# Twelve strided units normalised on GpSimd, and turn and values one unit step later

## The chip, the cores and the metric

One Trainium2 chip, one NeuronCore of it. The metric is the device time in microseconds (us) of one execution, as the median of several runs. Engines are named as the profile names them: PE (TensorE matmuls), PEld (its weight loads), DVE (VectorE), ACT (ScalarE), POOL (GpSimd), and the DMA queues that an engine issues to (SPq, ACTq, POOLq).

## The reference

Attention over 8 batches, 8 heads, 576 positions and 64 dimensions, then a mixture of 8 experts with one expert per token. All data is float32.

```
scores = (q @ k.T) / sqrt(64)
heads 0-3: key j is seen by query i if 0 <= i - j < 32             (local)
heads 4-7: key j is seen if j <= i and j % 32 == i % 32            (strided)
attn = exp(scores - max) / (sum + 1e-9);  x = attn @ v             (4608 tokens x 512)
logits = x @ w_gate + modality_bias[modality_id]
expert = argmax(logits);  gate = softmax(logits)[expert]
out = gate * (relu(x @ w1[expert]) @ w2[expert])                   (512 -> 1024 -> 512)
```

## The kernel before

The kernel has two stages on one core. The attention stage writes the 4608 rows of x to DRAM and works out where each token belongs; the expert stage gathers tokens in slots of 256 and runs the two expert layers on each slot.

**Units.** Attention is cut into 32 units that alternate: even units are local (one head of two batches), odd units are strided (two heads of one batch). Strided units count their own index from 0 to 15, so `self.n` of a strided unit is k for the unit 2k+1 of the loop. A unit goes through five parts:

- `load` and `load_values` (SP's queue, issued in program order, each made to follow a PE instruction named in `at`): q and k, then v.
- `prep` (local only): q is copied into a padded tile `qd`, one half by DVE, one half by ACT (L326).
- `masks` and `scores`: PE writes the mask and adds the score products in PSUM. DVE takes the maximum and subtracts it (L353 and L354 for local, L454 and L455 for strided), ACT takes the exponential (L355 and L356; L456). For a strided unit DVE then sums (`sms`, L458), adds 1e-9 (L459), takes the reciprocal (L460) and multiplies the exponentials by it into `en` (L462). Local units are divided after the value product instead.
- `turn`: PE transposes the exponentials (`ex` of a local unit, `en` of a strided one) and ACT copies them to SBUF (`et`, L368 and L371; `eb`, L471).
- `values`: PE multiplies by v. For a local unit DVE adds 1e-9, takes the reciprocal and scales into `xt` (L392 to L398); for a strided one ACT copies into `xc` (L491).

**The unit loop.** PE's instructions are kept in the order in which they are written (`manual_schedule`). Step n of the loop writes: masks and scores of unit n, turn of unit n-2, values of unit n-3, the loads of later units in between, `prep` of unit n+2, one store of finished rows (`store_rows`, a POOL DMA of L498 that is kept in order with the other POOL DMAs), and five pieces of the `extra` work (`pop(POPS)`): transposes of a finished pair of batches, its routing, and the slot tables. The other engines' orders are set by a planner that lists instructions by program order and by when it reckons them ready. An engine executes its list in order.

**Buffers.** PSUM is a ring of eight banks (`pa`). `ex`, `exs`, `sms`, the loaded tiles and `eb` have two buffers each, `et` one, and the `en` tiles two, kept by hand in `ens` because their padding is zeroed once by POOL.

After the loop the local pool is released and the expert stage's tiles are laid over it. Its slots are gathered by POOL's indirect DMAs and its weights are converted by ACT and DVE beside the matmuls of L940 and L954.

Of the kernel before, what the change touches and what calls it, by code (L numbers as in the profile page):

```python
# [11 lines left out]
F32 = mybir.dt.float32  # L12
# [5 lines left out]
ALU = mybir.AluOpType  # L18
AX = mybir.AxisListType

P = 128
# [51 lines left out]
def _place(g, jj):  # L73

    return 16 + jj if g == 8 else 4 * (g // 2) + g % 2 + 2 * jj
# [7 lines left out]
def _residues(half, a, j):  # L83

    return (16 * half + 6 * a + 3 * j, 3) if a < 2 else (16 * half + 12 + 2 * j, 2)
# [106 lines left out]
def attention_moe(ctx: ExitStack, tc: tile.TileContext, a, out):  # L192
    nc = tc.nc
# [15 lines left out]
    def keep_busy(n, name):  # L209
        t = pa(name)  # L210
        for _ in range(n):
            nc.tensor.matmul(t, idle[:, 0:P], idle[:], start=True, stop=True)  # L212
# [11 lines left out]
    at = {"scores": None, "turn": None, "values": None}  # L224
# [63 lines left out]
    lp = lp_cm.__enter__()  # L288


    def zeros(n, shape, name):
        return [lp.tile(shape, F32, bufs=1, name=f"{name}{i}") for i in range(n)]

    qds = zeros(2, [P, 18, 2, 32], "qd")
    ets = zeros(1, [P, 18, 2, 32], "et")
    ens = zeros(2, [P, 12, 64], "en")
    for t in qds + ets:
        nc.vector.memset(t[:], 0.0)
    for t in ens:
# [3 lines left out]
    class Local:  # L303
# [34 lines left out]
        def scores(self):  # L338
            n, qk, qd = self.n, self.qk, self.qd
            mx = lp.tile([P, 9], F32, tag="mx", name=f"mx{n}")  # L340
            self.ex = ex = lp.tile([P, 11, 64], F32, tag="ex", name=f"ex{n}")
            for g0, gn, s in self.ss:
                for g in range(gn):
                    for jj in range(2):
                        i = _place(g0 + g, jj)
                        at["scores"] = nc.tensor.matmul(  # L346
                            s[64 * jj:64 * jj + 64, g, :],
                            qd[:, i, :, :].rearrange("p b q -> p (b q)"),
                            qk[:, 18 + i:20 + i, :].rearrange("p b q -> p (b q)"),
                            start=False, stop=True, skip_group_check=True,  # L350
                        )
                m = mx[:, g0:g0 + gn]
                nc.vector.tensor_reduce(m, s, AX.X, ALU.max)  # L353
                nc.vector.tensor_tensor(ex[:, g0:g0 + gn, :], s, m.unsqueeze(2).to_broadcast([P, gn, 64]), ALU.subtract)  # L354
                nc.scalar.activation(ex[:, g0:g0 + 4, :], ex[:, g0:g0 + 4, :], AF.Exp, scale=0.125)  # L355
            nc.scalar.activation(ex[:, 9:11, :], ex[:, 8:9, :].to_broadcast([P, 2, 64]), AF.Exp, scale=0.125)  # L356
# [46 lines left out]
    class Strided:  # L403
# [30 lines left out]
        def scores(self):  # L434
            n, qk = self.n, self.qk
            for sl in range(6):
                for j in range(2):
                    r0, nr = _residues(sl % 2, sl // 2, j)
                    w, c = 18 * nr, slice(18 * r0, 18 * r0 + 18 * nr)
                    for h in range(2):  # L440
                        r = slice(64 * h, 64 * h + 64)
                        at["scores"] = nc.tensor.matmul(
                            self.s[h][64 * j:64 * j + w, 54 * sl:54 * sl + w], qk[r, 0, c], qk[r, 1, c],
                            start=False, stop=True, skip_group_check=True,
                        )
            mx = lp.tile([P, 12], F32, tag="mxs", name=f"mxs{n}")
            ex = lp.tile([P, 12, 54], F32, tag="exs", name=f"exs{n}")

            def bc(t, k):
                return t.unsqueeze(2).to_broadcast([P, k, 54])  # L450

            for h in range(2):
                s3, g = self.s[h].rearrange("p (i k) -> p i k", i=6), slice(6 * h, 6 * h + 6)
                nc.vector.tensor_reduce(mx[:, g], s3, AX.X, ALU.max)  # L454
                nc.vector.tensor_tensor(ex[:, g, :], s3, bc(mx[:, g], 6), ALU.subtract)  # L455
            nc.scalar.activation(ex[:], ex[:], AF.Exp, scale=0.125)  # L456
            sm = lp.tile([P, 12], F32, tag="sms", name=f"sms{n}")
            nc.vector.tensor_reduce(sm[:], ex[:], AX.X, ALU.add)  # L458
            nc.vector.tensor_scalar(sm[:], sm[:], 1e-9, None, ALU.add)  # L459
            nc.vector.reciprocal(sm[:], sm[:])  # L460
            self.en = ens[n % 2]
            nc.vector.tensor_tensor(self.en[:, :, 0:54], ex[:], bc(sm, 12), ALU.mult)  # L462

        def turn(self):
            n = self.n
# [29 lines left out]
    def store_rows():  # L495
        if rows:
            dst, src = rows.pop(0)
            pin(nc.gpsimd.dma_start(dst, src))  # L498

    def finish_pair(bp, xt, xcs):  # L500

        def rows_of(c, k0):
            kn = min(4, 9 - k0)
            t = pa(f"xs{bp}{c}{k0}").rearrange("p (g q) -> p g q", g=4)
            for k in range(kn):
                turned_to(t[:, k, :], xcs[2 + c][:, P * (k0 + k):P * (k0 + k + 1)])
            nc.scalar.copy(xt[:, k0:k0 + kn, 256 + P * c:256 + P * c + P], t[:, :kn, :])  # L507

        def columns_of(c, k0):
            kn = min(4, 9 - k0)  # L510
            t = pa(f"xl{bp}{c}{k0}").rearrange("p (g q) -> p g q", g=4)
            for k in range(kn):
                turned_to(t[:, k, :], xt[:, k0 + k, P * c:P * c + P])
            nc.scalar.copy(xcs[c][:, P * k0:P * (k0 + kn)], t[:, :kn, :].rearrange("p g q -> p (g q)"))

        def store(k, kn):
            r0 = T2 * bp + P * k
            rows.append((xd[r0:r0 + P * kn, :].rearrange("(k p) c -> p k c", p=P), xt[:, k:k + kn, :]))

        for c in range(2):  # L520
            for k0 in (0, 4, 8):
                yield
                columns_of(c, k0)
        routing = route(bp, xt, xcs)
        next(routing)
        next(routing)
        for k0 in (0, 4, 8):
            for c in range(2):
                next(routing, None)
                yield  # L530
                rows_of(c, k0)
                if k0 and c == 0:
                    store(k0 - 2, 2)
            store(k0, min(2, 9 - k0))
        yield from routing
# [448 lines left out]
    units, ends = [], {}  # L984
# [10 lines left out]
    def after(bp, xt, xcs):  # L995
        yield from finish_pair(bp, xt, xcs)
        yield
        for ph, (last_bp, _) in enumerate(PHASES):
            if bp == last_bp:
                yield from slots(ph)  # L1000

    extra = []

    def pop(k):
        for _ in range(k):
            while extra and next(extra[0], extra) is extra:
                extra.pop(0)
# [15 lines left out]
    def look_up(k):  # L1023
        if k == len(plan):
            found[k] = half_entries()
        if k < len(plan) and plan[k][1] in tables:
            n, t, s, xrows = plan[k]
            found[k] = entries(n, tables[t][0], s, xrows)
# [13 lines left out]
    nu = len(units)  # L1042
# [4 lines left out]
            units[i].prep()  # L1047
    man = tc.manual_schedule(engines={mybir.EngineType.PE})
    man.__enter__()
    for n in range(nu + 3):  # L1050
        paced = n >= PACED

        if not paced:
            for part in range(2):
                if n + 3 < nu:
                    units[n + 3].load(part, None)
            for part in range(2):
                if 1 <= n <= nu:
                    units[n - 1].load_values(part, None)
        if n in FILL:  # L1060
            keep_busy(FILL[n], f"warm{n}")
        if paced and n + 3 < nu:
            units[n + 3].load(0, at["values"])
        if n < nu:
            units[n].masks()
            units[n].scores()
        if paced and n + 3 < nu:
            units[n + 3].load(1, at["scores"])
        if 2 <= n <= nu + 1:
            units[n - 2].turn()  # L1070
        if paced and n <= nu:
            units[n - 1].load_values(0, at["turn"])
        if n >= 3:
            units[n - 3].values()
            if n - 3 in ends:
                extra.append(after(*ends[n - 3]))
        if paced and n <= nu:
            units[n - 1].load_values(1, at["values"])
        if n == SETUP:
            routing_setup()  # L1080
        if n + 2 < nu:
            units[n + 2].prep()
        store_rows()
        pop(POPS)
        for i in range(2):
            if n == nu - 4:
                look_up(i)
            if n == nu - 3:
                gather(i)
            if n == nu - 2:  # L1090
                load(0, i)
        if n == nu + 1:
            turn(0)
    man.__exit__(None, None, None)
    lp_cm.__exit__(None, None, None)
# [68 lines left out]
```

## Time and profile before

| what | value |
| --- | --- |
| median of 3 runs | 603.1 us (601.81 to 607.35) |
| the profiled execution, and its span | 602.83 us, 601.0 us |
| granted clock, mean | 0.993 |
| busy share of the span | PE 94%, PEld 83%, DVE 74%, ACT 65%, POOL 42% |
| moved by DMA | 102.46 MB, mean 170 GB/s |

A busy share is a mean over both stages. A row of the stretches view gives, for a stretch of the span, the busy time of each engine; a row of the timeline gives start, duration, engine, line, tiles and, in brackets, how long the engine sat idle before it and what ended that. In the timeline rows that are merged, xN counts the instructions.

### The profile page before, as it was taken

What the parts mean: (1) busy time and instruction counts of PE and PEld (TensorE: products, weight loads), DVE (VectorE), ACT (ScalarE), POOL (GpSimd) and SP (SyncE); (2) the same over time, 40 slices, a digit from 0 to 9 for tenths busy, and PEclk for the clock granted to TensorE, in tenths of its full rate; (3) what the DMA queues carried; (4) which work ended last, traced back from release to release, by engine and by line L of the source; (5) the groups of instructions that cost most, each with busy time, mean ns of one, the idle gap of its engine ahead of it and who ended that gap; (6) DMA issues with size and microseconds to landing.
All of it is one profiled execution on the core that took longest, in us unless ns stands there. A gap on an engine that the chain in (4) does not pass through costs nothing.

```text
span 601.0 us, 15492 instructions
## 1 busy us (share of the span) xinstructions
PE 565.7 (94%) x6107; PEld 498.5 (83%) x6109; DVE 446.8 (74%) x1076; ACT 388.6 (65%) x798; POOL 250.4 (42%) x226
## 2 busy tenths in 40 slices
PE   8777899797899999999999999999999999999995
PEld 4666787676669999999999999999999999999994
DVE  7867886985968799666787787787787787787542
ACT  4767877765796666776665575575665665665652
POOL 0011011117237537555645645645645646532310
PEclk9999899999999999999999999999999999999998
DMA  8984997998844944744754743313214239413621
GB/s 311 299 259 152 335 316 257 322 306 273 267 115 164 219 168 105 217 170 106 177 210 106 219 167 93 71 36 105 72 37 106 70 116 277 111 40 72 228 103 41
DMA packets 73572, 102.46 MB, mean 170 GB/s; under 512 B 48531, under 2 KB 48787, under 8 KB 69908
## 3 DMA queue, kind: packets, MB, share of 16 engines
q0 software_dynamic: 20672, 58.01, 28.6%
q1 hardware_dynamic: 52340, 42.87, 26.8%
q8 instruction: 50, 0.82, 0.6%
q10 hardware_dynamic: 480, 0.51, 0.3%
q14 instruction: 30, 0.25, 0.1%
HBM read 123.85 MB, written 19.18 MB: 238 GB/s over the span
## 4 chain that ended last, share of the span: by engine, by line
PE 82%; ACT 7%; DVE 6%; issue 3%; POOL 0%; another core or an unknown queue 0%; POOLq 0%; ACTq 0%
PE h L940 34%; PE o L954 33%; PE o L382 2%; PE s L346 2%; PE ot L483 1%; ACT xc L491 1%; PE lg L543 1%; PE xs L227 1%; PE ts L227 1%; DVE ex L354 1%; DVE mx L353 1%; DVE sms L458 1%; PE t L227 1%; PE warm L212 1%; ACT et L368 1%
## 5 line engine op out<-in xcount | busy, mean ns | idle before, releaser
L976 DVE TENSOR_TENSOR wl<-raw,wh 128x512 fp32r<-128x512 f32 x288 | 187.7, 691 | 64.2 <-ACT wh L975 55.2
L975 ACT CAST wh<-raw 128x512 fp32r<-128x512 f32 x288 | 163.9, 619 | 66.6 <-PE o L954 43.1
L940 PE MATMUL h<-xh,wl 128*128 128x256 f32 x576 | 162.7, 283 | 0.0
L940 PE MATMUL h<-xl,wh 128*128 128x256 f32 x576 | 162.6, 283 | 0.0
L940 PE MATMUL h<-xh,wh 128*128 128x256 f32 x576 | 162.4, 282 | 0.1
L822 POOL DMA_INDIRECT raw<-in_w,wi x72 | 95.9, 1332 | 156.3 <-DVE wl L976 117.6
L940 PEld LDWEIGHTS h<-xh,wh 128*128 128x128 f32 x576 | 109.5, 190 | 7.5 <-issue 0.6
L940 PEld LDWEIGHTS h<-xl,wh 128*128 128x128 f32 x576 | 109.6, 190 | 5.5
L954 PE MATMUL o<-wh,hh 128*128 128x512 f32 x288 | 114.2, 396 | 0.0
L954 PE MATMUL o<-wl,hh 128*128 128x512 f32 x288 | 113.8, 395 | 0.0
L940 PEld LDWEIGHTS h<-xh,wl 128*128 128x128 f32 x576 | 109.7, 190 | 1.4 <-DVE wl L976 0.4
L954 PE MATMUL o<-wh,hl 128*128 128x512 f32 x288 | 110.5, 391 | 0.0
L943 ACT ACTIVATE hh<-h 128x256 fp32r<-128x256 f32 x144 | 55.4, 385 | 71.1 <-PE h L940 46.7
L945 DVE SCALAR_TENSOR_TENSOR hl<-h,hh 128x256 fp32r<-128x256 f32 x144 | 60.7, 421 | 33.3 <-ACT hh L943 21.6
L954 PEld LDWEIGHTS o<-wh,hl 128*128 128x128 f32 x288 | 53.5, 188 | 11.0
L954 PEld LDWEIGHTS o<-wh,hh 128*128 128x128 f32 x288 | 54.6, 189 | 7.6
L954 PEld LDWEIGHTS o<-wl,hh 128*128 128x128 f32 x288 | 54.6, 190 | 5.6
L962 POOL DMA_INDIRECT out<-y,le x36 | 44.7, 1242 | 20.6 <-ACT y L961 11.0
L806 POOL DMA_INDIRECT fx<-xd,le x36 | 40.1, 1113 | 11.9 <-issue 10.7
L813 POOL DMA_INDIRECT le<-ld,li x36 | 39.4, 1095 | 12.9 <-issue 10.1
L498 POOL DMA_DIRECT2D xd<-xt x20 | 14.5, 727 | 62.3 <-ACT xt L507 62.3
L382 PE MATMUL o<-vv,et 128*64 128x65 f32 x512 | 22.7, 231 | 5.5 <-issue 3.3
(189 smaller groups left out, 749.1 us busy)
## 6 DMA issues: line engine op xcount, KB each, us to landing
vv<-in_vl SPq DMA_DIRECT2D x32, 292.5 KB
qks<-in_qks SPq DMA_DIRECT2D x32, 288.0 KB
xd<-xt POOLq DMA_DIRECT2D x16, 512.0 KB
qk<-in_qkl SPq DMA_DIRECT2D x16, 304.0 KB
qk<-in_qkl SPq DMA_DIRECT2D x16, 288.0 KB
vs<-in_vs SPq DMA_DIRECT2D x32, 144.0 KB
raw<-in_w,wi POOLq DMA_INDIRECT x72
xd<-xt POOLq DMA_DIRECT2D x4, 256.0 KB
```

The costliest lines, as they stand in the source:

```text
L227: at["turn"] = nc.tensor.transpose(dst, src, ident)
L382: at["values"] = nc.tensor.matmul(o[64 * jj:64 * jj + 64, k, :], et[:, u, :, :].rearrange("p g q -> p (g q)"), vv[:, u, :], start=True, st ...
L806: pin(nc.gpsimd.indirect_dma_start(xt[:, h, :], None, xd[0:xrows, :], IOA(ap=le[:, h, 0:1], axis=0)))
L813: pin(nc.gpsimd.indirect_dma_start(le[:, h, :], None, ld[0:xrows, :], IOA(ap=li[:, s, h:h + 1], axis=0)))
L822: pin(nc.gpsimd.indirect_dma_start(raws[j].rearrange("p f c -> p (f c)"), None, a["w"], IOA(ap=wi[:, s, j:j + 1], axis=0), bounds_check=E ...
L940: nc.tensor.matmul(hp, w[:, a1], x[:, c, :], start=(k == 0), stop=(k == 11))
L943: nc.scalar.activation(hh[:], hp, AF.Relu)
L945: nc.vector.scalar_tensor_tensor(hl[:], hp, 0.0, hh.bitcast(F32), ALU.max, ALU.subtract)
L954: nc.tensor.matmul(os[h], hx[:, m], w[:, 512:1024], start=(f == 0 and i == 0), stop=(f == 7 and i == 2))
L962: outs.add(pin(nc.gpsimd.indirect_dma_start(out, IOA(ap=le[:, h, 0:1], axis=0), y[:], None, bounds_check=NT - 1, oob_is_err=False)))
L975: nc.scalar.copy(wh[:, c], raw[:, c])
L976: nc.vector.tensor_tensor(wl[:, c], raw[:, c], wh[:, c].bitcast(F32), ALU.subtract)
```

## The change

Four things are edited. The multiplication into `en` (L462) goes to GpSimd for the strided units whose index is under 12 (loop units 1 to 23) and stays on VectorE for the last four. In step n the loop turns unit n-3 instead of n-2, multiplies by the values of unit n-4 instead of n-3, and loads the values of unit n-2 instead of n-1. The loop has one more step (36 instead of 35), and the turn of the first expert slot moves with it. `en` and the local `ex` have three buffers instead of two.

```
-    ens = zeros(2, [P, 12, 64], "en")
+    ens = zeros(3, [P, 12, 64], "en")
...
-            self.ex = ex = lp.tile([P, 11, 64], F32, tag="ex", name=f"ex{n}")
+            self.ex = ex = lp.tile([P, 11, 64], F32, tag="ex", bufs=3, name=f"ex{n}")
...
-            self.en = ens[n % 2]
-            nc.vector.tensor_tensor(self.en[:, :, 0:54], ex[:], bc(sm, 12), ALU.mult)
+            self.en = ens[n % 3]
+            (nc.gpsimd if n < 12 else nc.vector).tensor_tensor(
+                self.en[:, :, 0:54], ex[:], bc(sm, 12), ALU.mult)
...
-    for n in range(nu + 3):
+    for n in range(nu + 4):
...
-                if 1 <= n <= nu:
-                    units[n - 1].load_values(part, None)
+                if 2 <= n <= nu + 1:
+                    units[n - 2].load_values(part, None)
...
-        if 2 <= n <= nu + 1:
-            units[n - 2].turn()
-        if paced and n <= nu:
-            units[n - 1].load_values(0, at["turn"])
-        if n >= 3:
-            units[n - 3].values()
-            if n - 3 in ends:
-                extra.append(after(*ends[n - 3]))
-        if paced and n <= nu:
-            units[n - 1].load_values(1, at["values"])
+        if 3 <= n <= nu + 2:
+            units[n - 3].turn()
+        if paced and n <= nu + 1:
+            units[n - 2].load_values(0, at["turn"])
+        if n >= 4:
+            units[n - 4].values()
+            if n - 4 in ends:
+                extra.append(after(*ends[n - 4]))
+        if paced and n <= nu + 1:
+            units[n - 2].load_values(1, at["values"])
...
-        if n == nu + 1:
+        if n == nu + 2:
             turn(0)
```

## Rows read from the trace of the kernel before

**Rows 1.** Stretches: busy PE, PEld, DVE, ACT, POOL; clock, DMA share, GB/s.
```profile
8.00:34.00 26.00, 20.87 (x603) 17.41 (x604) 22.10 (x58) 19.18 (x42) 1.13 (x4) 1.00 0.91 294
...
34.00:58.00 24.00, 18.29 (x431) 14.46 (x429) 16.72 (x45) 15.81 (x36) 1.52 (x3) 1.00 0.71 226
58.00:127.00 69.00, 60.02 (x1584) 51.81 (x1580) 58.09 (x216) 52.29 (x118) 11.10 (x16) 0.98 0.91 296
127.00:171.00 44.00, 36.28 (x724) 28.92 (x723) 34.11 (x132) 30.40 (x70) 17.29 (x19) 1.00 0.78 265
171.00:601.00 430.00, 423.46 (x2732) 382.79 (x2730) 311.53 (x620) 268.78 (x532) 218.86 (x180) 0.99 0.45 128
```
**Rows 2.** Timeline of PE: the strided turns that waited, and one score.
```profile
15.54 0.84 PE L227 MATMUL ts<-cf_sb,en 128*128 128x128 f32 x6 [0.73 <-DVE en L462]
...
22.53 0.85 PE L227 MATMUL ts<-cf_sb,en 128*128 128x128 f32 x6 [1.22 <-DVE en L462]
...
24.65 1.45 PE L346 MATMUL s<-qk,qd 128*64 128x64 f32 x36
...
30.37 0.85 PE L227 MATMUL ts<-cf_sb,en 128*128 128x128 f32 x6 [1.94 <-DVE en L462]
...
71.22 1.54 PE L227 MATMUL ts<-cf_sb,en 128*128 128x128 f32 x6 [0.89 <-DVE en L462]
...
108.90 0.88 PE L227 MATMUL ts<-cf_sb,en 128*128 128x128 f32 x6 [1.47 <-DVE en L462]
...
152.57 0.87 PE L227 MATMUL ts<-cf_sb,en 128*128 128x128 f32 x6 [0.69 <-DVE en L462]
```
**Rows 3.** Timeline of ACT, from 19 us and from 33 us.
```profile
19.78 1.19 ACT L368 COPY et<-t 64x512 f32<-64x512 f32 x2 [2.01 <-PE t L227]
...
23.60 0.67 ACT L326 COPY qd<-qk 64x576 f32<-64x576 f32 x1
...
38.35 0.42 ACT L355 ACTIVATE ex<-ex 128x256 f32<-128x256 f32 x1 [5.04 <-DVE ex L354]
```
**Rows 4.** The chain of work that ended last, 30 to 60 us.
```profile
35.05 1.24 DVE en L462
...
45.85 0.83 DVE en L462
```
**Rows 5.** Timeline of DVE around one reciprocal of a strided unit.
```profile
85.44 0.22 DVE L460 RECIPROCAL sms<-sms 128x12 f32<-128x12 f32 x1
...
85.92 0.43 DVE L326 COPY qd<-qk 64x576 f32<-64x576 f32 x1
86.28 0.82 DVE L462 TENSOR_TENSOR en<-exs,sms 128x648 f32<-128x648 f32 x1
```
**Rows 6.** Timeline of DVE: one addition of 1e-9, and the last work before 74.7 us.
```profile
34.20 0.55 DVE L459 TENSOR_SCALAR sms<-sms 128x12 f32<-128x12 f32 x1
...
74.18 0.45 DVE L624 TENSOR_TENSOR hb<-cf_sb,pbf 128x288 bf16<-128x288 f32 x1
```
**Rows 7.** Timeline of POOL, 30 to 120 us.
```profile
34.05 0.67 POOL L270 TENSOR_TENSOR bias<-nmod,rt_sb 128x288 f32<-128x288 f32 x1
34.80 0.80 POOL L271 TENSOR_TENSOR bias<-bias,bias 128x288 f32<-128x288 f32 x1
58.31 1.73 POOL L498 DMA_DIRECT2D xd<-xt  x2 [22.71 <-ACT xt L507]
...
74.72 1.15 POOL L633 TENSOR_TENSOR hv<-hb,val 128x576 f32<-128x576 bf16 x1 [9.05 <-DVE hb L624]
```
**Rows 8.** One line's instructions: ns, least/median/most.
```profile
L459 DVE TENSOR_SCALAR sms<-sms x16: 160/164/547, 13.4 to 158.0; 128x12 f32<-128x12 f32 x16
...
L462 DVE TENSOR_TENSOR en<-exs,sms x16: 816/823/1237, 14.6 to 158.4; 128x648 f32<-128x648 f32 x16
...
L326 DVE COPY qd<-qk x16: 435/442/452, 5.7 to 137.5; 64x576 f32<-64x576 f32 x16
```
**Rows 9.** Timeline of PE in the loop's last steps.
```profile
157.06 1.04 PE L483 MATMUL ot<-eb,vs 54*64 54x54 f32 x48 [1.25 <-ACT et L368]
```

## The prediction

> **What bounds the kernel now.** I began with the stretches [rows 1]. From 171 us to the end TensorE is busy for 423.5 of 430 us, so the expert stage is TensorE's, and the change touches nothing in it. What can move is the attention stage, and it is to be read in four stretches because the limits differ. In 8 to 34 us (I call it I) TensorE is busy for 20.9 of 26 us, VectorE for 22.1, ScalarE for 19.2, and the DMA share is 0.91. In 34 to 58 us (II) none is full: 18.3, 16.7 and 15.8 of 24. In 58 to 127 us (III) TensorE has 60.0, VectorE 58.1 of 69, DMA again 0.91. In 127 to 171 us (IV) TensorE has 36.3 of 44. TensorE is thus idle for about 28 us in all between 8 and 171, and nobody else is full: the stage is a ring of engines that wait for each other. A step of the unit loop takes about 163/35 = 4.7 us (8 to 171 us over the loop's 35 steps).
>
> Next the timeline of TensorE, for what ends its waits. Six strided turns wait for VectorE's `en`: 0.73, 1.22, 1.94, 0.89, 1.47 and 0.69 us, 6.9 us together [rows 2]. Three lie in I, two in III, one in IV, none in II. Then who is late behind them: ScalarE works from 19.78 us with no wait up to the copy of `qd` at 23.60, which ends at 24.27, and the scores that need it start at 24.65 [rows 2, 3]. In II the chain of waits runs through `en` itself, once for 1.24 and once for 0.83 us, and ScalarE stood idle for 5.04 us for VectorE between the two [rows 3, 4].
>
> **The change, part by part.**
>
> *One step more before the turn.* A strided turn gets some 4.7 us more after its exponentials, and all six waits end. What is gained is what the next late thing leaves. In I the first (0.73) and third (1.94) go whole; of the second only 24.65 - 24.27 = 0.38 goes, since `qd` comes no sooner. That is 3.05 us. ScalarE and VectorE, at 74% and 85% of I, must have the room for it; if VectorE has not, I keep 0.4.
>
> *The multiplication leaves VectorE.* Twelve times 0.82 [rows 8] is 9.9 us less VectorE work. In II, units 7, 9 and 11, it lies on the chain: 1.24 + 0.83 = 2.1 us [rows 4], and ScalarE's 5.04 us wait for VectorE says that ScalarE can follow. I take 2.0. In I the same relief lies beside the waits already counted, so I add nothing.
>
> *It arrives on GpSimd, beside VectorE.* No row shows this instruction there. Its price by element from `hv` is 1.15/576 x 648 = 1.29 us, from the sum of the two biases 0.80/288 x 648 = 1.80 [rows 7]. I take 1.5, nearer to `hv`, whose size is nearest. The turn is a step away, so this duration itself is hidden; without that cover it would cost about 0.7 us a unit. But GpSimd's work is not free for VectorE. The addition of 1e-9 takes 0.16 us in the median and once 0.55: it started at 34.20 and ended at 34.75, and GpSimd's multiplication of the biases ran from 34.05 to 34.72 [rows 6 to 8]. The one `en` of 1.24 instead of 0.82 us, at 35.05, lies under the next GpSimd instruction, 34.80 to 35.60 [rows 4, 7, 8]. So some VectorE instructions are held until GpSimd is done. Which will meet the new one? After the reciprocal of a strided unit VectorE subtracts once more and then copies `qd`: reciprocal at 85.44 to 85.66, copy at 85.92 [rows 5]. This order stands in 7 of the twelve units (3, 5, 13, 15, 17, 21, 23). GpSimd starts 0.09 us after what it waits for (`hb` ends at 74.63, `hv` starts at 74.72) [rows 6, 7], hence at 85.75 here, and ends at 87.25. If the copy is held like the addition of 1e-9, it loses 1.33 us, against 0.82 saved: 0.51 worse for VectorE in each of 7 units, 0.82 better in 5, together -0.5 us instead of -9.9.
>
> The Trainium skill, page "SBUF — State Buffer", section "Who interferes with whom", has this as a rule that speaks against the change: a VectorE instruction with two SBUF inputs, or a copy, cast or tensor_scalar in a 2-port mode, contends for a port pair with GpSimd, and the later one blocks fully. By that rule the `qd` copies are held and the sum is mine; were they not, it would be about 593. The 0.55 and the 1.24 agree with it. The page "GPSIMD Engine Reference", section 3.1, measured a two-input float32 instruction at 1.96 times VectorE; estimated from that, 0.82 x 1.96 = 1.6 us, which makes each hold 0.1 longer.
>
> In III, units 13 to 23, five of six are held: 5 x 0.51 - 0.82 = 1.7 us more for VectorE; not held, 6 x 0.82 = 4.9 less. The two waits of TensorE that end there (0.89 + 1.47 = 2.4) work the other way. I take the held end, because the addition of 1e-9, like the copy, reads one SBUF tensor; 1.7 against 2.4 I call 0. Bounds for III: 4.9 gained to 1.7 lost.
>
> *One more step at the end.* TensorE's work is the same in sum, so the least cost is nothing. With scores gone, little stands between a turn and its values: one such pair shows 0.87 + 1.25 + 1.04 us with a 1.25 us wait for the copies of `et` [rows 2, 9], so the most is a whole round, 3.2 us. I take one such wait, 1.2, less the 0.69 that ends in IV: 0.5 lost.
>
> *At nothing.* The third buffers only loosen, and GpSimd's padding of the third `en` lies in its idle start. The loads of values and their place on SP's queue move by one step with their use; the same bytes pass per step. Unit 0's values now stand behind unit 5's q and k. No wait of TensorE in [rows 2] is for a load, and q and k are three units ahead; if that cover failed, one load of 585 KB at the 294 GB/s of I is 2.0 us. On GpSimd's queue the new instruction can be listed behind a store of rows that waits for ScalarE, as the first did until 58.31 [rows 7]. PE's turn waits behind it then, with masks, values and scores queued after that turn; the extra 4.7 us is the cover, and past it each microsecond of such a wait is one of TensorE's.
>
> **Sum.** Against the profiled execution of 602.83 us: -3.05 (I) - 2.0 (II) + 0 (III) + 0.5 (IV) = -4.5, so 598.3. The median, 603.1, is 0.3 above that execution; I leave that inside the range.
>
> **Rivals.**
>
> *Nothing comes of it, about 602.5.* The waits for `en` turn into others. The eight PSUM banks serve about six tiles a step, so a turn still reuses the banks of the scores of one step ago, which VectorE must have read, whatever the lag. For it: ScalarE's stretch without a gap behind the second wait, and DMA at 0.91. Against: 5.04 us of ScalarE waiting in II. Only 0.4 of I stays, II gives 0.4, the end takes 0.5.
>
> *The full relief, about 593.5.* The copies are not held, or the planner puts them elsewhere. Then III gives 4.9: 602.8 - 3.05 - 2.0 - 4.9 + 0.5 = 593.3. For it: no row shows a copy of `qd` under GpSimd's work. Against: 0.55 and 1.24; and DMA at 0.91 leaves III at most 9%, 6.2 us.
>
> *Slower, about 610.* VectorE is held after every reciprocal, by copies in some units and by the small routing instructions in others, each time for a GpSimd instruction of 1.80 us: the copy at 85.92 would start at 87.55, 1.63 later, net 0.81 a unit, 9.7 us for twelve. VectorE's delay then passes to TensorE through the PSUM ring, and II gives nothing: 602.8 + 9.7 - 3.05 + 0.5 = 610. It decides from where the holds, spread over the twelve, pass 0.82 + 2.5/12 = 1.03 us. For it: VectorE at 84% of III. Against: in five units nothing that resembles the held ones follows the reciprocal soon.
>
> **How the numbers follow.** Forecast 0.42, by itself 595 to 602; nothing 0.25; full relief 0.20; slower 0.13. The range takes in the full relief with a little of what lies past it, and stops short of the slower rival: 592 to 607. A measurement of this kernel tells from no change what passes about 1%, 6 us (its three runs lie 5.5 apart). Faster by over 1%, under 597: the full relief and somewhat over a third of the forecast, 0.36. Slower by over 1%, over 609: most of that rival, and a little for a wait on GpSimd's queue, 0.12. Within: 0.52.
>
> **What would show it.** Right: no TensorE wait for `en` above 0.2 us; TensorE busy in about the same time, with the expert stage's first matmuls some 4 us earlier; L462 on POOL at 1.3 to 1.8 us; `qd` copies on VectorE of up to 1.8 instead of 0.44 us, about seven of them. Wrong if these copies stay at 0.44 (then faster), if new waits for ScalarE's copies or VectorE's reads of PSUM take the place of `en` (then the same), or if the strided turns wait for POOL.

## The result, and the profile after

The changed kernel takes 609.57 us in the median of 20 runs (606.11 to 613.37), the kernel before 604.72 us (601.81 to 609.8). The ratio is 1.0082 with a 95% interval of 1.0063 to 1.0102: slower by some 5 us, where 598.3 was forecast, and above the range of 592 to 607. The profiled execution took 610.05 us with a span of 607.7 us and a mean granted clock of 0.975. A ratio is formed within one job, from undisturbed runs alone, and need not be the quotient of the two medians.

The stretches of the changed kernel, with the columns of [rows 1]:

```profile
8.00:34.00 26.00, 23.67 (x669) 19.14 (x665) 22.94 (x66) 20.44 (x46) 6.95 (x10) 1.00 0.98 311
34.00:58.00 24.00, 21.18 (x502) 17.83 (x501) 14.72 (x40) 17.50 (x40) 3.27 (x3) 0.93 0.78 244
58.00:127.00 69.00, 60.15 (x1491) 50.89 (x1490) 56.90 (x212) 50.18 (x116) 18.55 (x21) 0.95 0.92 295
127.00:171.00 44.00, 35.17 (x618) 27.36 (x618) 24.54 (x106) 21.67 (x51) 15.65 (x18) 0.81 0.67 225
```

Against [rows 1], 8 to 34 us did what was hoped: 669 matmuls in place of 603, TensorE busy for 23.67 of 26 us instead of 20.87. From 34 us on a new thing stands in the clock column: 0.93, 0.95 and 0.81, where the kernel before had 1.00, 0.98 and 1.00. From 127 to 171 us TensorE got through 618 matmuls instead of 724, and VectorE and ScalarE fell with it (24.54 and 21.67 instead of 34.11 and 30.40): whatever was late there, it was neither of these.

The stages are best compared up to the first expert matmul (L940 before, L941 after; 165.6 us before, 172.5 us after), since all that follows takes 435.4 and 435.2 us (601.0 - 165.6 and 607.7 - 172.5):

```profile
165.62 0.39 PE L940 MATMUL h<-xh,wh 128*128 128x256 f32 x1
```
```profile
172.46 0.39 PE L941 MATMUL h<-xh,wh 128*128 128x256 f32 x1
```

First the kernel before, then the changed one, from 8 us to that matmul:

```profile
8.00:165.60 157.60, 130.77 (x3285) 109.28 (x3284) 125.62 (x434) 112.27 (x253) 29.83 (x39) 0.99 0.86 283
```
```profile
8.00:172.50 164.50, 141.57 (x3285) 116.39 (x3281) 120.45 (x429) 111.29 (x253) 44.42 (x51) 0.92 0.84 271
```

The same 3285 matmuls are in both. TensorE's idle time fell from 157.60 - 130.77 = 26.83 to 164.50 - 141.57 = 22.93 us, by 3.9, but the time in which it counts as busy rose by 10.8. The two make the 6.9 us by which the expert stage starts later.

Where on the way? The scores of unit 28 start at 125.67 us, which were at 135.06 before. (Part of that lead is work put off, since a step later turn and values leave more to do behind it: 667 matmuls instead of 567.) From there to the first expert matmul, before and after:

```profile
135.10:165.60 30.50, 24.51 (x567) 20.13 (x563) 22.71 (x97) 18.73 (x44) 14.83 (x17) 1.00 0.82 272
```
```profile
125.70:172.50 46.80, 37.88 (x667) 29.76 (x663) 27.20 (x120) 24.47 (x57) 16.74 (x19) 0.82 0.68 225
```

24.51/567 is 43 ns a matmul, 37.88/667 is 57 ns, and TensorE idles for 8.9 us instead of 6.0. The loss lies here: 46.8 - 30.5 = 16.3 us longer, of which the 100 matmuls put off explain 100 x 43 ns = 4.3. Up to unit 28 the lead is 135.06 - 125.67 = 9.4 us, and 5.1 without the work put off. TensorE's timeline of the changed kernel shows how it begins (idle time ahead of an instruction, and what ended it, in brackets; "issue" means that TensorE waited for nothing that the profile shows):

```profile
125.67 1.22 PE L346 MATMUL s<-qk,qd 128*64 128x64 f32 x36
126.81 0.87 PE L227 MATMUL ts<-cf_sb,en 128*128 128x128 f32 x6
127.61 0.53 PE L382 MATMUL o<-vv,et 128*64 128x65 f32 x6
128.55 0.30 PE L382 MATMUL o<-vv,et 128*64 128x65 f32 x3 [0.41 <-issue]
...
132.87 0.38 PE L382 MATMUL o<-vv,et 128*64 128x65 f32 x4 [1.04 <-issue]
134.32 0.50 PE L382 MATMUL o<-vv,et 128*64 128x65 f32 x4 [1.07 <-issue]
...
136.01 3.64 PE L544 MATMUL lg<-xc,rt_sb 128*32 128x256 f32 x32
```

The value products of unit 24 come in small groups of three to six, one group in some 0.7 us and in 1.4 us towards the end, and take from 127.61 to 134.75 us. Then the 32 matmuls of `lg` take 3.64 us (1.93 in e18, one of the experiments below). In stretches of 3 us the same place reads:

```profile
129.00:132.00 3.00, 1.46 (x19) 0.97 (x19) 0.49 (x1) 0.42 (x1) 2.36 (x3) 1.00 0.94 371
132.00:135.00 3.00, 1.07 (x9) 0.82 (x9) 0.80 (x3) 2.08 (x5) 0.94 (x1) 0.76 0.88 320
135.00:138.00 3.00, 3.00 (x25) 1.67 (x28) 1.42 (x5) 0.82 (x3) 0.00 (x0) 0.50 0.64 198
138.00:141.00 3.00, 3.00 (x32) 1.79 (x25) 0.00 (x0) 0.62 (x2) 0.00 (x0) 0.60 0.00 0
```

TensorE is busy for 1.46 and 1.07 of 3 us, with VectorE and ScalarE nearly empty beside it in the first of the two and the DMA share at 0.94 and 0.88. Then the granted clock falls from 2.4 to 1.2 GHz (0.50), and the work that follows runs at half speed. So the stretch pays twice, for the small groups and for the clock behind them. The Trainium skill, page "TensorE: Matmul & The Clock Gate", section "A second HAM failure mode: psum-queue depth-cycling", describes something near it: a kernel in which TensorE idles briefly and often between groups of matmuls while PSUM banks are cycled, and whose clock goes back and forth between the two levels. The 1.46 and 1.07 us followed by 0.50 agree.

Small groups are not new, though. The kernel before has them too, shorter, and its clock stays at 1.00:

```profile
138.49 0.28 PE L483 MATMUL ot<-eb,vs 36*64 36x36 f32 x3 [0.45 <-issue]
139.22 0.32 PE L483 MATMUL ot<-eb,vs 36*64 36x36 f32 x3 [0.45 <-issue]
```
```profile
138.00:141.00 3.00, 1.87 (x16) 1.43 (x15) 0.00 (x0) 1.24 (x5) 2.39 (x3) 1.00 0.82 271
```

From 125 to 152 us its waits for "issue" add up to some 4 us, those of the changed kernel to 5.6. Nor is unit 24 the whole loss. The experiment e1 below (on chip 11) runs the same instructions on TensorE in the same order without this loss. Cut at the same place in that order (the first strided mask after unit 28, at 141.6 and 133.2 us), the two halves are, for the changed kernel and then for e1:

```profile
125.70:141.60 15.90, 11.87 (x137) 8.00 (x133) 5.96 (x21) 6.95 (x17) 5.93 (x6) 0.79 0.63 211
141.60:172.50 30.90, 26.00 (x531) 21.75 (x530) 21.24 (x99) 17.51 (x41) 10.81 (x13) 0.83 0.70 232
```
```profile
124.70:133.20 8.50, 7.98 (x139) 6.02 (x133) 5.66 (x21) 6.70 (x17) 5.94 (x6) 1.00 0.81 300
133.20:158.20 25.00, 22.21 (x531) 19.08 (x530) 19.70 (x94) 17.55 (x41) 10.98 (x13) 0.93 0.86 291
```

7.4 us are lost by 141.6 us and 5.9 more after it, where the clock of the changed kernel is down a second time.

The parts that I had costed, in the changed kernel. By line, `en` (L462) on GpSimd and on VectorE:

```profile
L462 POOL TENSOR_TENSOR en<-exs,sms x12: 1262/1272/1274, 14.4 to 108.7; 128x648 f32<-128x648 f32 x12
L462 DVE TENSOR_TENSOR en<-exs,sms x4: 825/833/835, 117.8 to 159.4; 128x648 f32<-128x648 f32 x4
```

Two copies of `qd` that met GpSimd's instruction, in the timelines of VectorE and GpSimd:

```profile
20.14 0.68 DVE L326 COPY qd<-qk 64x576 f32<-64x576 f32 x1
34.19 0.85 DVE L326 COPY qd<-qk 64x576 f32<-64x576 f32 x1
```
```profile
19.23 1.27 POOL L462 TENSOR_TENSOR en<-exs,sms 128x648 f32<-128x648 f32 x1 [3.59 <-DVE rs L392]
33.45 1.27 POOL L462 TENSOR_TENSOR en<-exs,sms 128x648 f32<-128x648 f32 x1
```

Both copies last until GpSimd is done or a little past it (20.82 against 20.50, 35.04 against 34.72), as the one held addition did before [rows 6, 7]. They are two, not seven. But copies are not all that is held. Four small routing instructions on VectorE met a multiplication too; those on GpSimd started at 60.54, 71.44, 99.21 and 108.71 us:

```profile
60.58 1.26 DVE L574 TENSOR_TENSOR lo<-lo,bias 128x8 f32<-128x8 f32 x1
...
71.72 1.01 DVE L594 TENSOR_SCALAR sml<-sml 128x9 f32<-128x9 f32 x1
...
99.61 0.95 DVE L577 TENSOR_TENSOR lo<-lo,mxl 128x72 f32<-128x72 f32 x1
...
108.93 1.08 DVE L594 TENSOR_SCALAR sml<-sml 128x9 f32<-128x9 f32 x1
```
```profile
60.54 1.27 POOL L462 TENSOR_TENSOR en<-exs,sms 128x648 f32<-128x648 f32 x1 [10.60 <-DVE lo L573]
...
108.71 1.26 POOL L462 TENSOR_TENSOR en<-exs,sms 128x648 f32<-128x648 f32 x1 [6.82 <-DVE pai L617]
```

They take 0.15, 0.16, 0.22 and 0.16 us where nothing holds them, and each ends within 0.1 us of GpSimd's. So these four lose 3.6 us and the two copies 0.65. On TensorE, strided turns that waited in [rows 2], and what waits now:

```profile
16.32 0.88 PE L227 MATMUL ts<-cf_sb,en 128*128 128x128 f32 x6
22.63 0.87 PE L227 MATMUL ts<-cf_sb,en 128*128 128x128 f32 x6
...
68.13 0.33 PE L334 MATMUL s<-cb_sb 128*64 128x320 bf16 x2 [1.27 <-DVE exs L455]
...
106.01 0.33 PE L334 MATMUL s<-cb_sb 128*64 128x320 bf16 x2 [1.27 <-DVE exs L455]
```

No turn waits for `en` any more. Two waits of 1.27 us for VectorE's read of a PSUM bank have come in 58 to 127 us.

### The profile page after: what moved, and what is told of

Read it like the earlier page. It is cut to its first block, busy times and chain, and to the rows that moved or that the text cites. A ratio compares the mean times of both kernels' runs of the same rounds, so it can differ in the third digit from the quotient of the medians.

```text
span 607.7 us, 15544 instructions
## 1 busy us (share of the span) xinstructions
PE 575.8 (95%) x6109; PEld 505.4 (83%) x6109; DVE 441.9 (73%) x1064; ACT 389.5 (64%) x798; POOL 257.2 (42%) x239
## 4 chain that ended last, share of the span: by engine, by line
PE 82%; DVE 7%; issue 4%; DMA 3%; ACT 3%; POOL 0%; POOLq 0%; SPq 0%; ACTq 0%
PE h L941 34%; PE o L955 33%; PE s L346 2%; DMA vv<-in_vl 2%; PE o L382 2%; PE ts L227 2%; PE lg L544 2%; PE xs L227 1%; PE xl L227 1%; PE ot L484 1%; DVE ex L354 1%; DMA qk<-in_qkl 1%; DVE sms L458 1%; PE t L227 1%; DVE mx L353 1%
## 5 line engine op out<-in xcount | busy, mean ns | idle before, releaser
L941 PE MATMUL h<-xh,wl 128*128 128x256 f32 x576 | 162.7, 283 | 0.0
L941 PE MATMUL h<-xl,wh 128*128 128x256 f32 x576 | 162.6, 283 | 0.0
L941 PE MATMUL h<-xh,wh 128*128 128x256 f32 x576 | 162.4, 282 | 0.1
L823 POOL DMA_INDIRECT raw<-in_w,wi x72 | 87.8, 1219 | 165.5 <-DVE wl L977 127.0
L941 PEld LDWEIGHTS h<-xh,wh 128*128 128x128 f32 x576 | 109.5, 190 | 7.5 <-issue 0.6
L941 PEld LDWEIGHTS h<-xl,wh 128*128 128x128 f32 x576 | 109.6, 190 | 5.5
L941 PEld LDWEIGHTS h<-xh,wl 128*128 128x128 f32 x576 | 109.6, 190 | 1.4 <-DVE rt L761 0.4
L963 POOL DMA_INDIRECT out<-y,le x36 | 44.4, 1233 | 20.7 <-ACT y L962 11.0
L462 POOL TENSOR_TENSOR en<-exs,sms 128x648 f32<-128x648 f32 x12 | 15.2, 1269 | 79.3 <-DVE sms L460 26.2
L807 POOL DMA_INDIRECT fx<-xd,le x36 | 40.1, 1115 | 11.0 <-issue 10.7
L814 POOL DMA_INDIRECT le<-ld,li x36 | 39.3, 1091 | 12.8 <-issue 10.4
L382 PE MATMUL o<-vv,et 128*64 128x65 f32 x512 | 24.8, 237 | 8.1 <-issue 7.0
```

The lines of the kernel that those rows point to most:

```text
L382: at["values"] = nc.tensor.matmul(o[64 * jj:64 * jj + 64, k, :], et[:, u, :, :].rearrange("p g q -> p (g q)"), vv[:, u, :], start=True, st ...
L807: pin(nc.gpsimd.indirect_dma_start(xt[:, h, :], None, xd[0:xrows, :], IOA(ap=le[:, h, 0:1], axis=0)))
L814: pin(nc.gpsimd.indirect_dma_start(le[:, h, :], None, ld[0:xrows, :], IOA(ap=li[:, s, h:h + 1], axis=0)))
L823: pin(nc.gpsimd.indirect_dma_start(raws[j].rearrange("p f c -> p (f c)"), None, a["w"], IOA(ap=wi[:, s, j:j + 1], axis=0), bounds_check=E ...
L941: nc.tensor.matmul(hp, w[:, a1], x[:, c, :], start=(k == 0), stop=(k == 11))
L963: outs.add(pin(nc.gpsimd.indirect_dma_start(out, IOA(ap=le[:, h, 0:1], axis=0), y[:], None, bounds_check=NT - 1, oob_is_err=False)))
```

## The experiments

Eighteen kernels ran in five jobs. The kernel before, timed beside them, has medians of 599.89 us (e1 to e4), 605.95 (e5 to e8), 607.26 (e9 to e12), 605.6 (e13 to e16) and 600.02 (e17, e18). The records name the chip: 11, 8, 10, 8 and 1. The same kernel thus differs by 1.2% between jobs on different chips (the two on chip 8 agree to 0.1%), and only kernels of one job are compared directly.

**The two parts alone, and the weight loads later** (chip 11, three rounds). e1 is the changed kernel with all multiplications on VectorE, e2 the kernel before with twelve of them on GpSimd:

```
e1, from after:   (nc.gpsimd if n < 12 else nc.vector).tensor_tensor(  ->  nc.vector.tensor_tensor(
e2, from before:  nc.vector.tensor_tensor(  ->  (nc.gpsimd if n < 12 else nc.vector).tensor_tensor(
```

> The changed kernel with all sixteen multiplications back on VectorE: the later turn and values and the third buffers alone. Clock theory (the change leaves TensorE with longer gaps, its granted clock falls, and the work at the lower level is the loss): if the later turn makes the gaps, 606 to 610 us at a mean granted clock of 0.985 or less; if GpSimd makes them, 602 to 605 at 0.99. Holding theory (GpSimd's multiplication holds VectorE): 598 to 603, since nothing holds. Theory of the extra step (one more step of the loop costs by itself): 607 to 611 whatever the clock.

> The kernel before with the twelve multiplications on GpSimd alone: old turn, old values, old buffers. Clock theory: 601 to 606 us, clock above 0.985, unless the waits of TensorE for the slower multiplication (1.27 instead of 0.82 us, now on the path) make new gaps. Holding theory: 606 to 611. Theory of the extra step: 601 to 605.

e1: 596.66 us, ratio 0.9935 (0.9904 to 0.9965). e2: 601.79 us, 1.0013 (0.9968 to 1.0059). In e1 unit 28's scores start at 124.69 us, 1.0 from the changed kernel's, and on TensorE and SP both run the same instructions in the same order. But the value products of unit 24 go through at once, and behind unit 28 the expert stage is reached in 33.5 us instead of 46.8:

```profile
126.64 0.69 PE L382 MATMUL o<-vv,et 128*64 128x65 f32 x16
127.15 0.29 PE L388 MATMUL o<-vv,et 128*64 128x65 f32 x4
127.27 0.64 PE L382 MATMUL o<-vv,et 128*64 128x65 f32 x16
```
```profile
124.70:158.20 33.50, 30.19 (x669) 25.10 (x663) 25.36 (x115) 24.25 (x57) 16.92 (x19) 0.95 0.85 293
```

Read alone, this says that the later turn gains 3.9 us and GpSimd's part loses the rest. That reading fell later. Two raw weight loads of the first expert slot are issued at 125.8 and 127.2 us in the changed kernel, just ahead of the small groups, so e3 (from after) and e4 (from before) made them follow the values of step 30:

```
-                load(0, i)
+                load(0, i, at["values"])      # handed down to follow(dma, last) in weights()
```

> The changed kernel in which the first two weight loads of the expert stage (1 MB each, at 125.8 and 127.2 us) follow the values of the loop's step 30, so that they no longer meet the loads of the last units. Clock theory: the gap of TensorE at 128 to 135 us and the low clock behind it are gone, mean granted clock 0.985 or more, 602 to 606 us. Holding theory and theory of the extra step: 608 to 612, no change.

> The kernel before with the same later weight loads. Clock theory: it has one short low clock only, at 70 us, far from the weight loads, so 600 to 605, at most 3 us faster. If late weights help the kernel before as much as the changed one (4 us or more), then meeting loads are a cost that both pay and not the loss of the change.

e3: 603.01 us, 1.0035 (1.0002 to 1.0069). e4: 604.53 us, 1.0062 (1.0027 to 1.0096). The kernel before loses by it; whether the changed one gains can't be said from this job, since it wasn't among the four. e3 has no small groups at unit 24, but its profiled execution still needs 41.1 us from unit 28 (128.4 us) to the expert stage, at a mean clock of 0.97 where the clock theory asked for 0.985; it was the slowest of its ten executions (606.81 us).

**How many multiplications move, and useless work in the last steps** (chip 8, three rounds). e5, e6 and e7 move six, eleven and all sixteen; e8 adds some 4 us of useless matmuls in steps 28 and 31 to 33:

```
e5 / e6 / e7:  n < 12  ->  n < 6 / n < 11 / n < 16
e8:            FILL = {2: 4, 3: 6}  ->  {2: 4, 3: 6, 28: 5, 31: 5, 32: 5, 33: 5}
```

> The changed kernel with the first six strided units on GpSimd instead of twelve. The later turn alone was 0.65% faster than before, the change as a whole 0.8% slower, so GpSimd's part costs 1.5%, about 9 us, in the presence of the later turn. Holding theory (each GpSimd multiplication costs VectorE some 0.75 us): half of that, a ratio to before of 1.001. Coincidence theory (the loss is TensorE's wait for instructions and data in the loop's last steps, and the low clock behind it, set off by when the units arrive there and not by how many multiplications moved): no proportion, near 0.994 or near 1.008, and the loss, if any, lies after unit 24.

> The changed kernel with eleven strided units on GpSimd. Holding theory: 1.007. Coincidence theory: anything between 0.99 and 1.01, following the clock and the waits after unit 24.

> The changed kernel with all sixteen on GpSimd, the last four behind the row stores and the gathers of the first slots on its queue. Holding theory: 1.013. Coincidence theory: no proportion, 0.99 to 1.01.

> The changed kernel with five useless 128 x 512 bfloat16 matmuls more at the start of the loop's steps 28, 31, 32 and 33, 4 us of extra TensorE work. Clock theory (much of the loss is work done at the lower clock in these steps): the mean granted clock rises to 0.985 or more, and the time is no longer than the change's, 1.000 to 1.008 of before, in spite of the extra work. If the clock is a symptom and the waits are the loss: 1.011 to 1.016, that is 2 to 5 us more.

e5: 1.0045 (1.0012 to 1.0078). e6: 1.0064 (1.0032 to 1.0095). e7: 0.997 (0.9932 to 1.0008). e8: 1.0085 (1.0048 to 1.0122). A cost that each moved instruction brings would put e7 highest; it is lowest. e5 and e8 fall between the bands of their theories. e8 neither helped nor, as far as can be seen across jobs, hurt. In the profiles of e5, e6 and e8 the value products of unit 24 wait for "issue" 2.5 us or more in sum. In e7 they don't; its small groups come later and elsewhere (waits from 125 to 152 us: total, times, longest):

```profile
PE ot L484 <- issue: 2.9, 5, 1.1
PE lg L549 <- issue: 1.0, 1, 1.0
```

**The place in TensorE's stream** (chip 10, three rounds). TensorE's instructions are the same from e1 to the changed kernel, so a wait bound to a place in its stream could be moved by more instructions at the start. The 13 useless matmuls of 512 columns there became 52 of 128 or 78 of 85, in the changed kernel (e9, e10) and in e1 (e11, e12):

```
-            nc.tensor.matmul(t, idle[:, 0:P], idle[:], start=True, stop=True)
-    keep_busy(WARM, "warm")
+            nc.tensor.matmul(t[:, 0:w], idle[:, 0:P], idle[:, 0:w], start=True, stop=True)
+    keep_busy(52, "warm", 128)                # or 78, 85
```

> The changed kernel, but the 13 useless matmuls of 512 columns at the very start are 52 of 128 columns: the same columns of useless work, 39 matmuls more ahead of the first mask, every later instruction on every engine unchanged. Theory 1 (where PE stands in its own instruction stream when it waits for nothing that the profile shows): the gaps of 0.3 to 2.2 us come at other instructions, by about 39 matmuls sooner, the trickling value products at 128 to 135 us go or move, and the time comes anywhere from 0.994 to 1.009 of the kernel before. Theory 2 (GpSimd's twelve multiplications delay the last steps whatever the place): the gaps may move, the sum of them between 8 and 171 us stays at 12 to 13 us, and the time stays at 1.006 to 1.010.

> The changed kernel with 78 matmuls of 85 columns at the start in place of 13 of 512: 65 matmuls more. Theory 1: gaps at yet other instructions, time between 0.994 and 1.009 and not the same as with 52. Theory 2: 1.006 to 1.010.

> Only the later turn and the third buffers (all sixteen multiplications on VectorE), with 52 matmuls of 128 columns at the start in place of 13 of 512. Without the 39 extra matmuls it ran at 0.9935 with 5.0 us of gaps in which PE waited for nothing shown. Theory 1: that was partly a lucky place; the gaps come to 8 to 13 us and the time to 0.997 to 1.006. Theory 2: the place does not matter, 0.991 to 0.996.

> As the one before, with 78 matmuls of 85 columns at the start. Theory 1: 0.994 to 1.006, by its gaps. Theory 2: 0.991 to 0.996.

e9: 1.0022 (0.9997 to 1.0047). e10: 1.0051 (1.0021 to 1.008). e11: 1.0042 (1.001 to 1.0073). e12: 1.0026 (1.0002 to 1.0051). All four times fall in theory 1's bands and outside theory 2's (the interval of e10 reaches into the latter), but theory 1's mechanism doesn't hold either: in all four profiles the small groups stay at the value products of unit 24, with 39 or 65 matmuls more ahead of them. (The Trainium skill, page "Runtime: NRT & Kernel Launch", section "Instruction fetch mechanics", says that the crossing of an instruction block is mostly hidden; that the groups did not move speaks with it.) What the job does show is that the later turn alone, without GpSimd, has the small groups too and is as slow. Either the chip or the shift had undone e1's gain.

**The same kernels on one chip** (chip 8, five rounds). e13 is the changed kernel and e14 is e1, both unaltered; e15 is e3 unaltered, and e16 is e1 with the edit of e3.

> The changed kernel once more, beside the later turn alone on one chip, since the two have so far been measured on different chips. Theory 1 (the last steps lose time where the value products of unit 24 meet the two raw weight loads, whoever multiplies, on chips where PE then goes on in small groups): 1.003 to 1.009, and within 0.003 of the later turn alone if that chip shows the small groups in both. Theory 2 (GpSimd's twelve multiplications lose it): 1.006 to 1.010, at least 0.010 above the later turn alone.

> The later turn and third buffers alone, all sixteen multiplications on VectorE, once more. Theory 1: 1.001 to 1.006 on a chip with the small groups between 126 and 136 us, and 0.992 to 0.996 on one without them. Theory 2: 0.991 to 0.996 either way.

> The changed kernel with the raw weight loads of the first expert slot made to follow the values of step 30, on the same chip as the two others. Theory 1: no small groups at 126 to 136 us, and 0.004 or more below the changed kernel beside it. Theory 2: the loads are not the cause, within 0.003 of the changed kernel.

> The later turn alone with the same later weight loads. Theory 1: 0.004 or more below the later turn alone, about the same as the changed kernel with late weights (within 0.003). Theory 2: as the later turn alone, 0.991 to 0.996, and 0.006 or more below the changed kernel with late weights.

e13: 608.0 us, 1.0044 (1.0014 to 1.0074). e14: 607.69 us, 1.0027 (1.0002 to 1.0051). e15: 607.63 us, 1.0038 (1.0014 to 1.0062). e16: 607.0 us, 1.0022 (0.9997 to 1.0047). Without any instruction moved to GpSimd, e14 shows what the changed kernel showed. Its timeline, and its stretch from unit 28's scores to the first expert matmul:

```profile
129.15 0.35 PE L382 MATMUL o<-vv,et 128*64 128x65 f32 x4 [0.40 <-issue]
...
134.96 0.52 PE L382 MATMUL o<-vv,et 128*64 128x65 f32 x5 [0.93 <-issue]
```
```profile
126.30:171.50 45.20, 36.32 (x668) 28.60 (x664) 27.15 (x120) 24.34 (x57) 16.73 (x19) 0.85 0.71 232
```

Theory 1 is another one here, that of the raw loads. The later loads did not buy what it asked for (0.004): e15 is 0.0006 below e13, e16 0.0005 below e14. That does not price the small groups at unit 24, though, because the moved loads are followed by a new wait. In e15 the value products behind them wait 5.75 us for their own load, in e16 5.07, and e13 and e14 have no such wait in their last steps:

```profile
158.11 1.81 PE L484 MATMUL ot<-eb,vs 54*64 54x54 f32 x48 [5.75 <-DMA vs<-in_vs]
```

In e16 the small groups leave unit 24 and come, ahead of the raw loads (from 144.4 us), at the scores of unit 30:

```profile
138.73 0.30 PE L346 MATMUL s<-qk,qd 128*64 128x64 f32 x2 [0.39 <-issue]
...
141.62 0.44 PE L346 MATMUL s<-qk,qd 128*64 128x64 f32 x6 [1.05 <-issue]
```

So small groups come without the raw loads ahead of them, and moving the loads moves the small groups without removing them.

**The kernel before, and all sixteen on GpSimd, again** (chip 1; three and five rounds). e17 is the kernel before, e18 is e7, both unaltered.

> The kernel before, against itself: 0.997 to 1.003, which says how far two samples of one kernel lie apart here. Its profile stands beside the others of this chip. If the later turn loses its gain behind unit 28 on this chip: unit 28's scores at 133 to 137 us, the first expert matmul 29 to 34 us later, against 125 to 128 and 44 to 46 in the kernels with the later turn. If instead this chip is slow in the last steps whatever the kernel: 38 us or more here too.

> All sixteen strided multiplications on GpSimd, once more (0.997 with an interval from 0.9932 to 1.0008 in three rounds). If it is what the others with the later turn are: 1.002 to 1.005, with the small groups of value products between 126 and 136 us. If the move of the last four really frees the last steps: 0.994 to 0.999, without the small groups there and with a tail of 36 to 40 us.

e17: 0.9995 (0.9958 to 1.0032). e18: 600.12 us, 1.0008 (0.9981 to 1.0035). Their stretches from unit 28's scores to the first expert matmul, e17 and then e18:

```profile
135.10:165.60 30.50, 25.17 (x570) 21.74 (x566) 23.95 (x102) 19.82 (x47) 14.80 (x17) 0.90 0.91 312
```
```profile
127.50:162.20 34.70, 31.81 (x666) 26.82 (x662) 24.55 (x103) 22.52 (x54) 18.43 (x20) 0.85 0.81 281
```

e17 repeats the 30.5 us of the kernel before to the tenth. e18 shows no small groups at unit 24 and gets there in 34.7 us. Its clock of 0.85 is as low as e14's with 10 us less, so a low clock in this stretch is not enough for the loss.

All profiled kernels with the later turn, side by side (first raw loads unmoved; the wait is that of `o` L382 for "issue" from 125 to 152 us):

| kernel | chip | on GpSimd | ratio | unit 28 to expert stage, us | wait at `o`, us |
| --- | --- | --- | --- | --- | --- |
| changed kernel | not recorded | 12 | 1.0082 | 46.8 | 4.0 |
| e13 (the same) | 8 | 12 | 1.0044 | 44.1 | 3.4 |
| e14 | 8 | 0 | 1.0027 | 45.2 | 3.1 |
| e5 | 8 | 6 | 1.0045 | 45.2 | 3.4 |
| e6 | 8 | 11 | 1.0064 | 44.4 | 4.3 |
| e8 (useless work added) | 8 | 12 | 1.0085 | 44.0 | 2.5 |
| e9, e10 | 10 | 12 | 1.0022, 1.0051 | 45.6, 45.1 | 3.0, 2.6 |
| e11, e12 | 10 | 0 | 1.0042, 1.0026 | 44.3, 45.6 | 2.9, 2.8 |
| e7 | 8 | 16 | 0.997 | 38.4 | none |
| e18 (the same) | 1 | 16 | 1.0008 | 34.7 | none |
| e1 | 11 | 0 | 0.9935 | 33.5 | none |

Where the value products of unit 24 come in small groups, the last steps take 44.0 to 46.8 us and the ratio is 1.0022 to 1.0085; where they don't, 33.5 to 38.4 us and 0.9935 to 1.0008. Each stretch and wait is read from one execution. The moved multiplications are not needed for the groups: e14, e11 and e12 have them with nothing moved.

**What the profiles have in common.** No kernel was run to test this, but the profiles show where small groups come. Let a train be two or more waits of TensorE for "issue" that start within 1.5 us of each other. Between 8 us and the expert stage every train starts and ends no more than 2.3 us after the start of one of GpSimd's indirect transfers: the raw loads, the gathers of `le` (L813 before, L814 after) or those of `fx` (L806, L807). Single waits stand elsewhere too. In the kernel before and in the changed one the gathers of `le` begin at

```profile
136.47 1.03 POOL L813 DMA_INDIRECT le<-ld,li  x1 [0.31 <-DVE mx L353]
```
```profile
128.47 0.98 POOL L814 DMA_INDIRECT le<-ld,li  x1 [0.31 <-issue]
```

All 14 kernels that were profiled on chips 8 and 10 and on the one not recorded have such trains, e7 among them; the six on chips 1 and 11 (e1 to e4, e17, e18) have the same transfers and no train. The long trains, of five to nine waits at unit 24, stand in the ten kernels among the 14 in which the gathers of `le` follow the raw loads within 0.4 us. In the kernel before there are 8 us between them, in e7 a multiplication on GpSimd (128.86 us) that the last four units bring there, and both have three waits at `le`; in e15 and e16 the raw loads come later, and there is none.

## Why the prediction was wrong

**The step that failed** is "One more step at the end": "TensorE's work is the same in sum, so the least cost is nothing", with a whole round, 3.2 us, as the most, and 0.5 taken. The work was the same (3285 matmuls), but its time was not: TensorE counted as busy for 10.8 us more up to the expert stage. From unit 28 on it is 13.4 us more (37.88 against 24.51), of which the 100 matmuls put off, at 43 ns, explain 4.3. In time the last steps lost 16.3 - 4.3 = 12.0 us where 0.5 was forecast. I had costed a wait for ScalarE's copies there and had no term for TensorE's own pace. Nor was the 1.25 us of [rows 9] a wait between a turn and its own values: it came behind the turn of the next unit. What the runs put in its place is a stretch in which TensorE goes on in small groups without a shown reason and then at 1.2 GHz.

**The waits for `en` (-3.05 and -2.0): right in kind.** All are gone, and idle time fell by 3.9 us in the changed kernel. The lead at unit 28 is 5.1 us without the work put off, where I and II together were forecast at 5.05. How much reached the end is seen only where the last steps stayed short: 0.9935 in e1, 3.9 us. On two other chips the same kernel, or its variants, came out at 1.0026 to 1.0042. So 4.5 us is a size that the chain of waits had room for, not one that every run gave.

**GpSimd's part (0 in 58 to 127 us): right in size, the reason partly.** The instruction took 1.27 us against 1.5 taken and 1.3 to 1.8 foreseen. Copies of `qd` are held, for 0.24 and 0.41 us rather than 1.33, and two rather than seven. In 58 to 127 us it was the small routing instructions that were held, which the prediction named only in its slower rival. Their 3.6 us against the 6 x 0.83 = 5.0 moved leave VectorE 1.4 us less there, where the forecast had 1.7 more. Over all twelve, 4.3 of 10.0 us are given back, and VectorE's busy time to the expert stage fell by 5.2. Yet no full relief came of that either. Alone it measured 1.0013 (e2); with the later turn, against the same kernel without it on the same chip, +0.0017 (e13 to e14), -0.0020 (e9 to e11) and +0.0025 (e10 to e12). The mean, 0.0007, is 0.4 us, less than any of the intervals.

**The rivals.** The slower rival named 610 and the time came to that, but not by its mechanism. It wanted VectorE held in each of the twelve units, by more than the move saves; it was held in six, VectorE's busy time to the expert stage fell from 125.62 to 120.45 us, and with all sixteen moved the kernel is not slower (0.997, 1.0008). "Nothing" was half right: waits of 1.27 us for VectorE's reads of PSUM did come, twice.

**The clock** was in no term of mine, though the page of the kernel before gave 0.993. It is no price by itself either: e17, an execution of the kernel before, had 0.977 and reached the expert stage at 165.6 us like the one with 0.993. It can cost where TensorE is busy without a break, as at 135 to 141 us of the changed kernel (3.00 of 3 us, twice).

**Open.** Why TensorE goes on in small groups. The place in its stream, the multiplications on GpSimd and the raw loads have each been moved without ending them. With the first raw loads unmoved, they stood at unit 24 in 9 of the 10 kernels with the later turn that were profiled on chips 8 and 10 (all but e7), and with later loads at unit 30 in both (e15, e16). On chips 1 and 11 none of the three had them at either place (e1, e18, and e3 with later loads). So the chip is a likely part of the cause. e7 is no exception to that: it has small groups at other work, beside the same gathers of GpSimd. Which property of a chip it would be, and whether the gathers bring the small groups or only come at the same time, nothing here tells: no kernel was run with the gathers alone moved. No version here is shown to beat the kernel before on more than one chip: e1's 0.9935 did not come again as e14.

## What to carry to other kernels

When a change removes waits of the engine that everything feeds, check afterwards that its idle time fell and its busy time for the same instructions stayed; the two together are the whole account, and here -3.9 and +10.8 told at once that the forecast mechanism worked and that something else was lost. A moved schedule also moves which work meets which transfers in the last steps, and that term can be as large as the gain. For effects under 1%, time the variants that are to be compared in one job on one chip: the first answer here (GpSimd loses 1.5%) came from two jobs and was wrong. And look for an unexplained wait in the kernel before as well: the small groups were there, shorter.

## What the runs showed of the hardware that was not expected

- The same program has medians of 599.9, 605.6 to 605.95, 607.3 and 600.0 us on chips 11, 8, 10 and 1.
- TensorE can go on in groups of three to six matmuls at intervals of 0.7 to 1.4 us, for 7 us, with no semaphore that the profile shows, beside a DMA share of 0.9; the granted clock fell to 1.2 GHz behind it. Trains of such waits stood beside GpSimd's indirect transfers in 14 of 14 kernels on some chips and in none of six on two others.
- GpSimd's float32 multiplication of 128x648 takes 1.27 us, 1.53 times VectorE's 0.83, and a VectorE copy that met it ended only 0.32 us after it, twice. Four small VectorE instructions that met it took 0.95 to 1.26 us instead of 0.15 to 0.22 and ended with it.
